# One product of 64 rows and 128 columns for two 64x64 products in a fused attention and MLP kernel

## The chip, the cores and the metric

The kernel runs on one core of a Trainium2 chip. The metric is the device time of one execution in microseconds. A core has a matrix engine (TensorE, PE in the profile), a vector engine (VectorE, DVE), a scalar engine (ScalarE, ACT), GpSimd (POOL) and a queue of transfers (SyncE, SP). A matrix product on TensorE is two instructions: a weight load, LDWEIGHTS, which puts the stationary operand into the 128x128 array (PEld in the profile), and MATMUL, which streams the columns of the moving operand through it (PE).

## What is computed

```python
q_n, k_n = rmsnorm(q, g_q), rmsnorm(k, g_k)            # (8, 12, 448, 64)
scores = matmul(q_n, k_n.T) / sqrt(64)
attn = exp(scores - max); attn = attn / sum(attn)
x = matmul(attn, v)                                    # -> (3584, 768)
h = x @ w_in                                           # first layer, 768 -> 2048
out = gelu_tanh(h) @ w_out                             # second layer, 2048 -> 768
```

There are 8 batches of 12 heads, 448 tokens and 64 values a head. Inputs and output are float32; the products are of bfloat16 operands with float32 sums.

## The kernel before

The kernel goes through the batches one after the other. For one batch it does an attention, which gives `xT` (768 by 448, transposed), and then the first layer with its gelu, which writes half of `g` (two batches of 448 tokens side by side). The second layer of tokens that are already in `g` is done in small pieces between the pieces of the next batch's attention, so that TensorE has work while ScalarE computes exponentials. Batch 0's attention is `first_attention`; batches 1 to 7 go through `attention(b, ...)`. What is left of the second layer after batch 7 is done in `final`.

Inside `attention` the order of TensorE's work is written out by hand in a string. A word `5r` takes five steps of the second layer; `u` is one unit of scores, `unit()` at L335; `s` is the sum of the exponentials by a product with ones, and `x` the product with `v`, both `products()` at L387. Batch 1 uses `SECOND`, batches 2 to 7 use `STEADY`:

```python
STEADY = (
    "5r u 11r uu 8r uu 8r 1r u 6r u 4r u 5r uu 6r su 5r u 3r u 2r 7r uxu 4r u 5r uu 1r s 7r u"
    " 3r uu 5r 16r x 11r s 5r x",
    ...
SECOND = (
    "u 8r uu 9r u 7r uu 10r u 3r u 5r u 2r u 4r us 6r u 3r u 1r u 6r xu 4r u 5r u 1r u"
    " 3r s 1r u 2r u 10r u 2r x 1r s 3r x",
```

Adjacent `r` words, such as `8r 1r`, make one run of steps. `STEADY` has 19 runs: it begins with one, right behind the first layer of the batch before, and each is followed by a `u`, an `s` or an `x`. `SECOND` has 22 runs, begins with a `u`, and each run is followed by a `u`, an `s` or an `x` too.

A unit makes the scores of 64 keys with 448 queries for two heads and two row halves: four products of 64 rows (the contraction) and 64 columns of stationary operand, each in its own quarter of the array. `products()` is cut in the same way. One step of the second layer (`quartered`, L495) is cut so too: the index `r` picks one half of the 128 contracted rows of block `f`, with its own output bank; the index `a` picks one half of the 128 tokens, with its own half of the output's partitions. The two products of one `r` have the same moving operand `wout[rs, f, lo:hi]`, of 384 or 192 columns. After all `f` the halves are swapped over the banks (`turn`), so each bank gets both halves of the contraction.

The first layer of batch 1 (`mm1_turn`, L537) is cut in the same way, with `xT` of 448 columns as the moving operand. The first layers of the other batches (L556 for batch 0, L625 and L652 for batches 2 to 7) and `final` (L914) use stationary operands of 128 rows and 128 columns. The profile writes these forms as 64\*64 and 128\*128. The transposes of batch 0 (L296) and the filler products (L269) are 128\*128 as well, and two small products for the gains (L1073) are 32\*128.

Of the kernel before, what the change touches and what calls it, by code (L numbers as in the profile page):

```python
# [17 lines left out]
def kernel(  # L18
# [11 lines left out]
    nc = tc.nc  # L30
    B, H, S, D = q.shape
# [7 lines left out]
    R = 64  # L39
# [23 lines left out]
    start = ctx.enter_context(ExitStack())  # L63
# [6 lines left out]
    def pair(name):  # L70
        rounds.append(rounds.pop(0))
        return rounds[-1]
# [34 lines left out]
    win = wts.tile([128, HP, d_ff], BF16)  # L107
    wout = wts.tile([128, nf, d_model], BF16)
# [5 lines left out]
    qT, xT = {}, {}  # L114
    g = gp.tile([128, nf, 2 * S], BF16, tag="g", name="g")
# [352 lines left out]
    def follows(mm):  # L468

        tc.add_manual_dep(  # L470
            nc.tensor.nop().ins, mm.ins.name,
            mybir.DependencyInfo(mybir.DependencyClass.Sync, mybir.DependencyReason.DATA),
        )

    def quartered(parts, finished, late=False):

        o = rounds.pop(0)
        half = nf // 2
        order = [(0, 0, nf), (1, 0, nf)]
        if late:
            order = [(0, 0, half), (1, 0, half), (1, half, nf), (0, half, nf)]
        steps = [(turn, f) for turn, lo, hi in order for f in range(lo, hi)]
        for n, (turn, f) in enumerate(steps):
            if n and turn != steps[n - 1][0]:
                follows(mm)
            for r in range(2):  # L490
                bank = (r + turn) % 2
                (i, lo, hi), rs = parts[bank], slice(r * D, (r + 1) * D)
                for a in range(2):
                    at = i * 128 + a * R
                    mm = nc.tensor.matmul(  # L495
                        o[a * R:(a + 1) * R, bank, :hi - lo], g[rs, f, at:at + R],
                        wout[rs, f, lo:hi],
                        start=(n == 0), stop=(n == len(steps) - 1),
                    )
            if n == len(steps) - 1:  # L500
                rounds.append(o)
                finished(o)
            yield
# [19 lines left out]
    def mm1_turn(b, i, turn, cs, begin=False, end=False):  # L523

        if begin:
            hs1[i] = [pair("hh"), None]
        elif hs1[i][1][0] != turn:
            follows(hs1[i][1][1])  # L530
        h = hs1[i][0]
        for c in cs:
            for r in range(2):
                j, rs = (r + turn) % 2, slice(r * D, (r + 1) * D)
                for a in range(2):
                    at = (2 * i + j) * 128 + a * R
                    mm = nc.tensor.matmul(  # L537
                        h[a * R:(a + 1) * R, j, :S], win[rs, c, at:at + R], xT[b][rs, c],
                        start=begin and c == cs[0], stop=end and c == cs[-1],
                    )  # L540
        hs1[i][1] = turn, mm
        if end:
            nc.scalar.activation(
                g[:, 2 * i:2 * i + 2, (b % 2) * S:(b % 2 + 1) * S], h[:, :, :S],
                AF.Gelu_apprx_tanh,
            )
# [182 lines left out]
    def attention(b, side, extra, ends):  # L729
# [12 lines left out]
        def second_layer():  # L742
            for k, parts in enumerate(tiles):
                def finished(o, k=k):
                    full[k] = o
                    made.add(("full", k))
                yield from quartered(parts, finished, late=b == 1 and k == 0)
# [76 lines left out]
        if b > 1:  # L824
            sevens[b] = Seven(b)
            sevens[b].early()
        else:
            mm1_turn(b, 0, 0, early, begin=True)
            mm1_turn(b, 1, 0, early, begin=True)
            mm1_turn(b, 0, 1, early)  # L830
            mm1_turn(b, 2, 0, early, begin=True)
            mm1_turn(b, 1, 1, early)
            mm1_turn(b, 2, 1, early)
# [237 lines left out]
    for j in range(2):  # L1071
        rs = slice(j * 32, (j + 1) * 32)
# [95 lines left out]
    for b in range(B):  # L1168
# [80 lines left out]
        for f in range((nf // 2, nf)[b] if b < 2 else 0):  # L1249
            i, part = f // 4 * 2, f % 4  # L1250
# [71 lines left out]
```

## Time and profile before

| | |
|---|---|
| median of 3 runs | 385.32 us (384.76 to 386.1) |
| the profiled execution's own time | 384.59 us |
| its span in the trace | 382.8 us |
| granted TensorE clock | 0.999 |
| busy share of the span: PE, PEld, DVE, ACT, POOL | 98%, 71%, 78%, 76%, 35% |
| TensorE instructions | 6508 MATMUL, 6508 LDWEIGHTS |
| of these L495, the second layer in the attentions | 3456 of each |
| of these L537, the first layer of batch 1 | 384 of each |

A busy matrix engine means that some product is in it; a product's record runs from its start until its last result is out, so records of products that follow each other overlap. How long a piece of work holds TensorE is therefore read from start to start, not from a record's duration.

### The profile page before, as it was taken

The page shows a single profiled execution, that of the slowest core. Times are in us where ns is not written, and L with a number is a line of the kernel's source. Part 1 is how long each engine was busy: PE and PEld are TensorE (multiplying, and loading weights), DVE is VectorE, ACT ScalarE, POOL GpSimd, SP SyncE. Part 2 cuts the span into 40 slices and gives each one's busy share as a digit, 9 for nine tenths or more (in the row PEclk, how much of TensorE's full clock was granted, in tenths as well). Part 3 has the DMA queues.
Part 4 walks back from the last instruction along what each step waited for, and adds up shares of the span by engine and source line. Part 5 has one row for each costly group of instructions (what it writes and reads, how often), then busy time and mean ns, then how long its engine had stood idle before and what let it go on. Part 6 is the DMA issues. An engine that isn't in the chain of part 4 may idle for free.

```text
span 382.8 us, 14538 instructions
## 1 busy us (share of the span) xinstructions
PE 374.9 (98%) x6508; PEld 273.6 (71%) x6508; DVE 299.4 (78%) x441; ACT 289.6 (76%) x358; POOL 134.1 (35%) x118
## 2 busy tenths in 40 slices
PE   8899999999999999999999999999999999999995
PEld 5565577677878858886678867788678866778563
DVE  4999969995999758895789956996588833899853
ACT  6995589777997689877897789966897659965500
POOL 5997504349203850057401861038400640000000
PEclk9999999999999999999999999999999999999999
DMA  8999999978913996259832897139553340220023
GB/s 255 324 236 210 210 238 235 275 152 190 245 48 77 223 203 112 59 109 260 184 90 53 193 252 117 45 89 222 112 98 84 74 96 15 74 63 3 2 61 105
DMA packets 64594, 54.48 MB, mean 142 GB/s; under 512 B 37652, under 2 KB 60436, under 8 KB 64532
## 3 DMA queue, kind: packets, MB, share of 16 engines
q1 hardware_dynamic: 54016, 41.04, 42.8%
q0 software_dynamic: 10128, 11.80, 18.5%
q8 instruction: 51, 0.84, 0.9%
q10 hardware_dynamic: 388, 0.72, 0.5%
q14 instruction: 11, 0.09, 0.1%
HBM read 45.61 MB, written 11.01 MB: 148 GB/s over the span
## 4 chain that ended last, share of the span: by engine, by line
PE 92%; ACT 5%; DMA 1%; DVE 0%; issue 0%; POOL 0%
PE t L495 33%; PE t L652 14%; PE t L625 13%; PE t L387 9%; PE t L335 8%; PE t L537 5%; PE t L914 5%; ACT ex L343 4%; PE t L556 4%; DMA rawq<-in_q_dram 1%; PE h L436 1%; PE tp L296 1%; PE o L387 0%; DVE ss L173 0%; POOL nrmq L278 0%
## 5 line engine op out<-in xcount | busy, mean ns | idle before, releaser
L343 ACT ACTIVATE ex<-t,shift 128x896 bf16<-128x896 f32 x168 | 156.7, 1013 | 2.9 <-PE t L335 2.2
L495 PE MATMUL t<-wout,g 64*64 64x384 bf16 (+1 forms) x3456 | 150.6, 305 | 0.0
L495 PEld LDWEIGHTS <-g 64*64 64x64 bf16 x3456 | 104.4, 107 | 29.2 <-issue 2.2
L335 PE MATMUL t<-qT,kT 64*64 64x448 bf16 x672 | 57.5, 351 | 1.4 <-ACT ex L343 0.6
L652 PE MATMUL t<-xT,win 128*128 128x448 bf16 x288 | 58.5, 353 | 0.0
L173 DVE TENSOR_REDUCE ss<-sq 128x14 f32<-128x896 f32 (+3 forms) x45 | 43.5, 995 | 18.5 <-ACT sq L162 16.1
L1035 POOL COPY mark<-es 1x1 bf16<-1x1 bf16 x7 | 1.2, 177 | 128.2 <-DVE es L362 119.8
L652 PEld LDWEIGHTS <-win 128*128 128x128 bf16 x288 | 27.7, 98 | 24.1 <-issue 2.1
L278 POOL TENSOR_TENSOR nrmq<-rawq,rinv 128x896 bf16<-128x896 f32 (+1 forms) x21 | 35.4, 1688 | 19.2 <-ACT rinv L205 10.6
L355 DVE TENSOR_TENSOR es<-ex 128x1792 bf16<-128x1792 bf16 x21 | 22.3, 1061 | 16.3 <-ACT ex L343 16.3
L278 POOL TENSOR_TENSOR nrmk<-rawk,rinv 128x896 bf16<-128x896 f32 (+1 forms) x21 | 34.6, 1647 | 0.0
L397 DVE STREAM_TRANSPOSE st<-t 128x448 f32<-128x448 f32 x42 | 24.8, 629 | 10.5 <-PE t L387 9.7
L387 PE MATMUL t<-ex,vb 64*64 64x448 bf16 x588 | 32.3, 350 | 0.0
L335 PEld LDWEIGHTS <-kT 64*64 64x64 bf16 x672 | 23.7, 106 | 9.4 <-issue 1.4
L625 PEld LDWEIGHTS <-win 128*128 128x128 bf16 x288 | 27.6, 98 | 2.7 <-issue 1.0
L658 ACT ACTIVATE g<-t 128x896 bf16<-128x896 f32 x24 | 22.0, 916 | 9.3 <-PE t L652 9.3
L387 PEld LDWEIGHTS <-vb 64*64 64x64 bf16 x672 | 23.3, 107 | 7.9 <-issue 1.2
L409 DVE STREAM_TRANSPOSE rb<-rc 128x896 f32<-128x896 f32 (+1 forms) x25 | 26.7, 1067 | 0.3
L636 ACT COPY xs<-t 128x896 f32<-128x896 f32 x18 | 16.3, 906 | 13.0 <-PE t L625 10.5
L422 DVE TENSOR_TENSOR xT<-t,rb 128x896 bf16<-128x896 f32 x21 | 22.8, 1086 | 0.9
L513 ACT COPY osb<-t 128x768 f32<-128x768 f32 (+1 forms) x18 | 12.6, 703 | 14.0 <-PE t L495 14.0
L164 POOL TENSOR_TENSOR sq<-rawk 128x896 f32<-128x896 f32 (+1 forms) x14 | 22.6, 1614 | 0.7 <-DMA rawk<-in_k_dram 0.7
(147 smaller groups left out, 529.3 us busy)
## 6 DMA issues: line engine op xcount, KB each, us to landing
rawq<-in_q_dram SPq DMA_DIRECT2D x22, 448.0 KB, 4.3
rawk<-in_k_dram SPq DMA_DIRECT2D x22, 448.0 KB, 5.7
out_dram<-osb SPq DMA_DIRECT2D x38, 192.0 KB, 2.9
vb<-in_v_dram POOLq DMA_DIRECT2D x6, 672.0 KB, 7.6
win<-in_moe_w_in_dram POOLq DMA_DIRECT2D x8, 384.0 KB, 11.6
out_dram<-osb SPq DMA_DIRECT2D x31, 96.0 KB, 2.5
wout<-in_moe_w_out_dram POOLq DMA_DIRECT2D x3, 768.0 KB, 18.0
vb<-in_v_dram POOLq DMA_DIRECT2D x2, 448.0 KB, 16.4
```

The source lines that it names most:

```text
L164: eng.tensor_mul(sq, raw, raw)
L173: nc.vector.reduce_sum(sss[b][:, seat(b, c), "qk".index(n), hs, ts], squares(b, c, n, hs, ts), axis=AX.X)
L278: eng.tensor_mul(nrms[n, b, c][:, ts].rearrange("p t a d -> p a t d"), raws[n, b, c][:, :, ts], root[:, :, ts].to_broadcast([P, 2, m, D]),)
L335: nc.tensor.matmul(sc[r * R:(r + 1) * R, a, :S], kT[rs, c, t, r], qT[b][rs, c, :, r], start=True, stop=True,)
L343: nc.scalar.activation(exs[b, c][:, t], scs.pop((b, c, t))[:, :, :S], AF.Exp, scale=scale, bias=shift)
L387: nc.tensor.matmul(o[r][a * D:(a + 1) * D], vb[b % 2][rs, 2 * c + a, i] if what else ones[rs], es[i][rs, a], start=(i == 0), stop=(i == n ...
L397: nc.vector.transpose(st[:, r].rearrange("p a b -> p (a b)"), o[r])
L409: nc.vector.transpose(oas["rb"][:, rs].rearrange("p r s -> p (r s)"), rc.to_broadcast([128, (rs.stop - rs.start) * m, 32]),)
L422: nc.vector.tensor_mul(xT[b][:, 2 * c:2 * c + 2], oas["o", c, 1][:, :, :S], oas["rb"])
L495: mm = nc.tensor.matmul(o[a * R:(a + 1) * R, bank, :hi - lo], g[rs, f, at:at + R], wout[rs, f, lo:hi], start=(n == 0), stop=(n == len(step ...
L625: nc.tensor.matmul(t[:, bank, n * QS:(n + 1) * QS], self.lhs[i][:, m, at:at + 128], self.rhs[i][:, m], start=i == owner and n == m == 0, s ...
L652: nc.tensor.matmul(h[:, j, :S], win[:, c, at:at + 128], xT[self.b][:, c], start=(c == 0), stop=(c == HP - 1),)
```

## The change

At two places the loop over `a` goes away. Where two products of 64 rows and 64 columns used the same moving operand, there is one product of 64 rows and 128 columns, which writes all 128 partitions of its bank. The loop over `r` stays, so a step is two products in place of four. The order of the steps among the units, sums and products, and all else, stays.

```diff
             for r in range(2):
                 bank = (r + turn) % 2
                 (i, lo, hi), rs = parts[bank], slice(r * D, (r + 1) * D)
-                for a in range(2):
-                    at = i * 128 + a * R
-                    mm = nc.tensor.matmul(
-                        o[a * R:(a + 1) * R, bank, :hi - lo], g[rs, f, at:at + R],
-                        wout[rs, f, lo:hi],
-                        start=(n == 0), stop=(n == len(steps) - 1),
-                    )
+                mm = nc.tensor.matmul(
+                    o[:, bank, :hi - lo], g[rs, f, i * 128:(i + 1) * 128], wout[rs, f, lo:hi],
+                    start=(n == 0), stop=(n == len(steps) - 1),
+                )
...
             for r in range(2):
                 j, rs = (r + turn) % 2, slice(r * D, (r + 1) * D)
-                for a in range(2):
-                    at = (2 * i + j) * 128 + a * R
-                    mm = nc.tensor.matmul(
-                        h[a * R:(a + 1) * R, j, :S], win[rs, c, at:at + R], xT[b][rs, c],
-                        start=begin and c == cs[0], stop=end and c == cs[-1],
-                    )
+                at = (2 * i + j) * 128
+                mm = nc.tensor.matmul(
+                    h[:, j, :S], win[rs, c, at:at + 128], xT[b][rs, c],
+                    start=begin and c == cs[0], stop=end and c == cs[-1],
+                )
```

The lines behind the edit move up: L495 becomes L493, L537 becomes L533, L556 becomes L552, L625 becomes L621, L652 becomes L648 and L914 becomes L910; L335 and L387 stay.

On TensorE, in batch 1's attention, a run of a single step (the word `1r` between two `u`) stands between two units. Before, with `t1` the output of the second layer, and `t3` and `t0` the scores of the unit ahead and the unit behind (the last part of a MATMUL row is the output's partitions by its columns):

```order
L335 MATMUL t3_894<-qT_845,kT_124 64x448
L495 LDWEIGHTS g_125
L495 MATMUL t1_101<-wout_120,g_125 64x384
L495 LDWEIGHTS g_125
L495 MATMUL t1_101<-wout_120,g_125 64x384
L495 LDWEIGHTS g_125
L495 MATMUL t1_101<-wout_120,g_125 64x384
L495 LDWEIGHTS g_125
L495 MATMUL t1_101<-wout_120,g_125 64x384
L335 LDWEIGHTS kT_124
L335 MATMUL t0_100<-qT_845,kT_124 64x448
```

The same place on TensorE after the change:

```order
L335 MATMUL t3_894<-qT_845,kT_124 64x448
L493 LDWEIGHTS g_125
L493 MATMUL t1_101<-wout_120,g_125 128x384
L493 LDWEIGHTS g_125
L493 MATMUL t1_101<-wout_120,g_125 128x384
L335 LDWEIGHTS kT_124
L335 MATMUL t0_100<-qT_845,kT_124 64x448
```

Four loads and four products of 64 columns became two loads and two products of 128 columns, at the same place between the same units; the units stay 64\*64.

Also on TensorE, batch 1's first layer begins right behind the last product with `v`. Before, with `t2` the layer's output:

```order
L387 LDWEIGHTS vb1_122
L387 MATMUL t1_101<-ex_1335,vb1_122 64x448
L537 LDWEIGHTS win_119
L537 MATMUL t2_893<-xT_1321,win_119 64x448
L537 LDWEIGHTS win_119
L537 MATMUL t2_893<-xT_1321,win_119 64x448
```

And after:

```order
L387 LDWEIGHTS vb1_122
L387 MATMUL t1_101<-ex_1207,vb1_122 64x448
L533 LDWEIGHTS win_119
L533 MATMUL t2_893<-xT_1193,win_119 128x448
L533 LDWEIGHTS win_119
L533 MATMUL t2_893<-xT_1193,win_119 128x448
```

The layer's four products of a step became two here too, and it now begins with a form that differs from the product ahead of it. At its other end a run of the second layer follows, whose form changed with it.

Counted over all of TensorE's program, two products that follow each other differ in form 36 times before: 17 times from 64\*64 to 128\*128, 17 times back, and once each way between 32\*128 and 128\*128. After, those stay (in 5 of them the 64\*64 is now 64 rows by 128 columns), and 267 changes between 64\*64 and 64 rows by 128 columns are new: 37 in each attention of batches 2 to 7 (19 at the ends of runs, 18 at the beginnings) and 44 in batch 1's, and 1 at the beginning of batch 1's first layer.

## The prediction

> **What bounds the kernel now.** The page's busy times come first, then its chain of waits.
>
> ```profile
> PE 374.9 (98%) x6508; PEld 273.6 (71%) x6508; DVE 299.4 (78%) x441; ACT 289.6 (76%) x358; POOL 134.1 (35%) x118
> PE 92%; ACT 5%; DMA 1%; DVE 0%; issue 0%; POOL 0%
> ```
>
> TensorE has a product in it for 98% of the span, and 92% of the chain that ended last lies on it. An average can hide a stage with another limit, so I read busy time by stretches: batch 4's attention, its first layer, batch 5's attention, then batch 1's attention and batch 1's first layer. The columns are the stretch, its length, and busy time with instruction counts for PE, PEld, DVE, ACT and POOL.
>
> ```profile
> 182.78:209.72 26.94, 26.94 (x694) 20.40 (x693) 22.58 (x31) 24.13 (x29) 3.90 (x5) 1.00 0.46 105
> 209.72:227.04 17.32, 17.32 (x136) 12.65 (x132) 12.58 (x15) 12.78 (x17) 12.38 (x9) 1.00 0.88 210
> 227.04:254.05 27.01, 27.01 (x694) 20.47 (x693) 22.65 (x31) 24.14 (x29) 3.97 (x5) 1.00 0.45 99
> 50.47:75.76 25.29, 25.29 (x581) 18.80 (x580) 22.51 (x40) 22.78 (x29) 6.67 (x8) 1.00 1.04 255
> 75.76:94.11 18.35, 18.35 (x391) 13.60 (x386) 15.46 (x27) 12.94 (x19) 12.66 (x9) 1.00 0.80 172
> ```
>
> TensorE is never empty in the stages that the change touches. ScalarE is next, with 24.13 us of 26.94. So time added on TensorE there has no cover and goes to the end of the kernel whole, and time removed there could bring at most 2.8 us an attention before ScalarE binds.
>
> Is TensorE also full, with columns streaming all the time? A busy record can't tell, so I take starts from the timeline (start, duration, line, form, count), first of a run in batch 4's attention, then of the final layer.
>
> ```profile
> 199.31 0.39 PE L335 MATMUL t<-qT,kT 64*64 64x448 bf16 x4
> 199.50 1.01 PE L495 MATMUL t<-wout,g 64*64 64x384 bf16 x20
> ```
>
> ```profile
> 359.98 1.30 PE L914 MATMUL t<-wout,g 128*128 128x384 bf16 x7
> ```
>
> The 20 products of L495 are five steps of four. The groups of the profile by line and form give one record's duration:
>
> ```profile
> L495 PE MATMUL t<-wout,g 64*64 64x384 bf16 x2688 | 132.4, 323 | 0.0
> L495 PE MATMUL t<-wout,g 64*64 64x192 bf16 x768 | 19.3, 243 | 0.0
> L914 PE MATMUL t<-wout,g 128*128 128x384 bf16 x48 | 8.3, 326 | 0.0
> L914 PE MATMUL t<-wout,vb 128*128 128x192 bf16 x16 | 1.5, 246 | 0.0
> ```
>
> Five steps lie within 1.01 us, of which the last four-product step takes about 0.36 (0.323 and a few hundredths between its first and last start), so a step is (1.01 - 0.36)/4 = 0.163 us. The full-array products of 384 columns come every (1.30 - 0.326)/6 = 0.162 us. A step of four quarter products thus already costs what one full-array product of that width costs: the quarters run beside each other, and the columns stream without a gap. The unit shows the same: 199.50 - 199.31 = 0.19 us for four products of 448 columns.
>
> **What the change removes.** It halves L495's 3456 and L537's 384 loads and products. Worth in time: next to nothing, since a step still streams 384 (or 192, or 448) columns. 864 steps of L495 could fall from 0.163 to the 0.162 of the full array, 0.9 us. TensorE's idle time ahead of L335, in all 1.4 us by the next row, is the only other slack. So the gain is between 0 and 2.3 us, and I take 0.
>
> ```profile
> L335 PE MATMUL t<-qT,kT 64*64 64x448 bf16 x672 | 57.5, 351 | 1.4 <-ACT ex L343 0.6 <-DVE kT L305 0.5 <-DVE shift L1083 0.3
> ```
>
> No trace shows a 64-row, 128-column product, so its step is bounded from both sides. If the two row halves run beside each other it is 0.162; one behind the other, 0.324. The nearest rows are the two 32\*128 products of L1073, in different row groups, in the timeline and then in the groups by form:
>
> ```profile
> 7.49 0.19 PE L1073 MATMUL t<-gbf,rows 32*128 32x32 bf16 x2 [0.66 <-DVE nrmq L278]
> 7.61 0.28 PE L296 MATMUL tp<-ident,nrmq 128*128 128x128 bf16 x2
> ```
>
> ```profile
> L1073 PE MATMUL t<-gbf,rows 32*128 32x32 bf16 x2 | 0.2, 184 | 0.7 <-DVE nrmq L278 0.7
> ```
>
> Both lie within 0.19 us although one takes 0.184, so they started together. I take 0.162.
>
> A load of 128 columns must also fit under a step. The narrow steps of 192 columns are the test, 192 of them (768 products by four). In the final layer a full-array product of 192 columns, each with its own 128-column load, comes every (1.5 - 0.246)/15 = 0.084 us, so the load keeps up. I take 0. The Trainium skill, "TensorE: Matmul & The Clock Gate", section "LDWEIGHTS (loading the stationary operand)", speaks against the change here: it prices a load by its columns at 1.2 a nanosecond, so 128 columns are 107 ns where 64 are 53. By that page alone, narrow steps paced by their load would cost 192 x (107 - 84) ns, an estimate of 4.4 us more; the row above, with loads of the same width at 84 ns, is against it.
>
> **What the change adds.** It puts 267 new changes of form on TensorE: 6 x 37 in the attentions of batches 2 to 7, 44 in batch 1's, and 1 into batch 1's first layer. What a change of form costs is seen where the trace has them. In batch 0's attention one unit (64\*64) and seven filler products (128\*128) alternate, and nothing waits for another engine between them:
>
> ```profile
> 10.89 0.38 PE L335 MATMUL t<-qT,kT 64*64 64x448 bf16 x4
> 11.21 0.58 PE L269 MATMUL o<-const-bfloat16-1.0 128*128 128x128 bf16 x7
> 11.72 0.38 PE L335 MATMUL t<-qT,kT 64*64 64x448 bf16 x4
> 12.04 0.58 PE L269 MATMUL o<-const-bfloat16-1.0 128*128 128x128 bf16 x7
> 12.55 0.38 PE L335 MATMUL t<-qT,kT 64*64 64x448 bf16 x4
> ```
>
> One round is 11.72 - 10.89 = 0.83 us. Its work, without changes, is 0.19 for the unit and 7 x 0.06 = 0.42 for the fillers (seven lie within 0.58, of which the last is 0.222 by the next row: 0.36/6 = 0.06). That leaves 0.83 - 0.61 = 0.22 us for two changes, 0.11 each.
>
> ```profile
> L269 PE MATMUL o<-const-bfloat16-1.0 128*128 128x128 bf16 x35 | 2.9, 222 | 0.0
> ```
>
> The unit alone tells it too: from its start to what comes behind is 11.21 - 10.89 = 0.32 us, against 0.19 in the run at 199.31, 0.13 more. At the beginning of batch 5's attention, where the full-array first layer gives way to the second layer, the timeline has
>
> ```profile
> 225.81 1.30 PE L652 MATMUL t<-xT,win 128*128 128x448 bf16 x6
> 227.04 1.01 PE L495 MATMUL t<-wout,g 64*64 64x384 bf16 x20
> 227.88 0.36 PE L335 MATMUL t<-qT,kT 64*64 64x448 bf16 x4
> ```
>
> Six products at the 0.19 that 448 columns take hold TensorE for 1.14 us; the run starts after 1.23, 0.09 more. The five steps behind take 0.84, where 5 x 0.163 is 0.82: the first step pays 0.02 to 0.03 on top, its weights not having been loaded beforehand. Together 0.115 us. The loads say why:
>
> ```profile
> 209.71 0.11 PEld L652 LDWEIGHTS <-win 128*128 128x128 bf16 x2 [0.36 <-issue]
> ```
>
> No load was issued for 0.36 us at the change, and the load starts only as the product does: TensorE empties first, and then nothing is ready.
>
> All these rows change the row count as well (64 to 128), and L1073 to L296 changes rows alone, from 32 to 128: 7.61 - 7.49 = 0.12 us for products of 32 columns, which is about 0.10 of emptying. None changes columns alone. So the price for 64\*64 against 64\*128 lies between 0 (if only rows matter) and 0.13. I take 0.115, between the round's 0.11 and the unit's 0.13, because the emptying is the same 0.09 to 0.11 whichever row counts change and in both directions. The Trainium skill, "TensorEngine Tiling (Array Packing)", section "Key Properties", says that a change of tiling mode drains TensorE while a change of tile doesn't, and lists 64x64 and 64x128 as different configurations; it gives no price, and the rows give one for other pairs only.
>
> The sum: 267 x 0.115 = 30.7 us, with no cover: 37 x 0.115 = 4.3 us in an attention of 26.94, which makes TensorE's lead over ScalarE wider. The other engines and the queue get later work, never earlier, and no wait is added. The profiled execution, 384.59 us, becomes 415.3. It lies 0.73 under the median of the runs, 385.32, so I forecast 416.0 us.
>
> **The rivals.** First, a change of columns alone is free. For it: no row shows such a change, and quarters that share rows are filled beside each other today. Against it: the steadiness of the price. It would give 385.3 less the 0 to 2.3 us above, 383.0 to 385.3: not slower. The price per change decides: below 1.2/267 = 0.004 us nothing is measured (0.3% of the time, 1.2 us, is about what a measurement can tell). 9%, of which 3% faster by over 0.3% and 6% within.
>
> Second, a partial price: TensorE needn't empty, but loads can't go ahead of a change, so each pays only the 0.02 to 0.03 of an unprepared first step: 267 x 0.025 = 6.7, 392.0 us. Against it is the 0.36 us without loads, which shows both at once. 8%.
>
> Third, the row halves don't run beside each other: 672 wide steps of 0.162, 192 of 0.084 and 96 of L537 at 0.19 are added, 109 + 16 + 18 = 143 us, and with the changes 559 us. The L1073 row is against it. 3%.
>
> **How the numbers follow.** The forecast has 80%. Its range: the price at its lowest reading, 0.09 x 267 = 24.0, less the gain of 2.3, is 384.6 + 21.7 = 406.3; at its highest, the whole 0.12 from L1073 to L296 and 0.025 for an unprepared step, 0.145 x 267 = 38.7, it is 423.3. With the median's offset, 407.0 to 424.0. The other cases lie outside it and hold the 20% that may be left out. Faster 0.03, same 0.06, slower 0.91.
>
> **What would show it.** In the changed profile, the run and the units around it should start 0.32 us behind a unit's start where it is 0.19 now; steps within a run should still be 0.163 apart; batch 4's attention should be about 31.2 us, batch 1's about 30.4, batch 1's first layer 18.4 to 18.5, and the full-array first layers unchanged at 17.3. Loads should pause at every change of form, and ScalarE should wait for L335. If attentions keep 27 us, the price is wrong; if steps are 0.32 apart, the overlap is.

## The result, and the profile after

The changed kernel takes 413.84 us (median of 4 runs, 413.7 to 414.0) where the kernel before takes 385.71 us in the same comparison: 1.073 times as long, 95% interval 1.071 to 1.076. Its profiled span is 412.0 us, 29.2 us over the span before.

The page's busy times and shares of the chain, after:

```profile
PE 403.3 (98%) x4588; PEld 227.7 (55%) x4588; DVE 301.9 (73%) x441; ACT 296.5 (72%) x358; POOL 134.2 (33%) x118
PE 92%; ACT 5%; DMA 1%; issue 1%; DVE 0%; POOL 0%; ACTq 0%
```

TensorE is as busy as before by share, with 1920 products fewer: busy time doesn't show that it now pauses 267 times more. The stretches do. These are batch 4's attention, its first layer, batch 1's attention and batch 1's first layer, with the columns as before.

```profile
195.04:226.17 31.13, 31.13 (x438) 15.03 (x437) 23.41 (x32) 25.30 (x29) 4.10 (x5) 1.00 0.38 87
226.17:243.50 17.33, 17.33 (x137) 12.66 (x134) 12.50 (x14) 12.66 (x17) 12.27 (x9) 1.00 0.87 219
50.07:79.95 29.88, 29.88 (x386) 12.72 (x385) 23.67 (x42) 23.58 (x29) 7.53 (x9) 1.00 0.92 219
79.95:98.12 18.17, 18.17 (x196) 9.35 (x194) 13.88 (x25) 12.88 (x18) 12.42 (x9) 1.00 0.74 176
```

An attention of batches 2 to 7 grew from the 27.01 us of the row before to 31.13, by 4.12; six of them make 24.7 us. For batch 1 the same ends, from first product to first product, give these rows before:

```profile
50.33:75.41 25.08, 25.08 (x578) 18.71 (x579) 22.30 (x40) 22.60 (x28) 6.32 (x8) 1.00 1.04 256
75.41:93.91 18.50, 18.50 (x391) 13.65 (x387) 15.81 (x27) 13.23 (x20) 12.81 (x9) 1.00 0.79 175
```

So batch 1's attention grew from 25.08 to 29.88, by 4.80. That is 4.12/37 = 0.111 us a change in the one and 4.80/44 = 0.109 in the other. The full-array first layer kept its 17.3 us, and batch 1's own first layer went from 18.50 to 18.17: before, one of its 96 steps took 0.53 us in place of 0.19, a pause that the changed kernel does not have. 24.7 + 4.8 - 0.3 is the whole 29.2 us; other stages differ by up to 0.3 us either way and cancel. The timeline shows where in an attention it lies; this is batch 4's, some 18 us in:

```profile
213.46 0.82 PE L493 MATMUL t<-wout,g 64*128 64x384 bf16 x8
214.21 0.38 PE L335 MATMUL t<-qT,kT 64*64 64x448 bf16 x4
214.53 0.99 PE L493 MATMUL t<-wout,g 64*128 64x384 bf16 x10
215.44 0.57 PE L335 MATMUL t<-qT,kT 64*64 64x448 bf16 x8
```

From the unit to the run behind it is 214.53 - 214.21 = 0.32 us, where it was 0.19. The run has five steps (10 products), and the next unit starts 0.91 us later, where five steps took 5 x 0.163 = 0.82. Within the run nothing changed: (0.99 - 0.33)/4 = 0.165 a step. The loads of the same place:

```profile
213.46 0.44 PEld L493 LDWEIGHTS <-g 64*128 64x128 bf16 x8 [0.36 <-issue]
214.21 0.11 PEld L335 LDWEIGHTS <-kT 64*64 64x64 bf16 x4 [0.32 <-issue]
214.53 0.60 PEld L493 LDWEIGHTS <-g 64*128 64x128 bf16 x10 [0.20 <-issue]
215.44 0.14 PEld L335 LDWEIGHTS <-kT 64*64 64x64 bf16 x8 [0.32 <-issue]
```

Each group of loads starts at the very time of its products and not ahead of them, with 0.20 to 0.36 us of no load in front, put down to no engine ("issue"). The groups by form show it as a sum, the first two rows before, the next two after:

```profile
L495 PEld LDWEIGHTS <-g 64*64 64x64 bf16 x3456 | 104.4, 107 | 29.2 <-issue 2.2
L335 PEld LDWEIGHTS <-kT 64*64 64x64 bf16 x672 | 23.7, 106 | 9.4 <-issue 1.4 <-DVE kT L305 1.2 <-DVE qT L309 0.2
L493 PEld LDWEIGHTS <-g 64*128 64x128 bf16 x1728 | 71.7, 94 | 65.8 <-issue 28.9 <-PE t L335 7.5 <-PE t L493 0.2
L335 PEld LDWEIGHTS <-kT 64*64 64x64 bf16 x672 | 17.4, 104 | 36.1 <-issue 32.7 <-DVE kT L305 1.2 <-DVE qT L309 0.2
```

The pauses of "issue" ahead of these loads went from 2.2 to 28.9 us and from 1.4 to 32.7. ScalarE now waits for the units too (first row before, then after), and the wide products' own records are as long as those of the quarters were:

```profile
L343 ACT ACTIVATE ex<-t,shift 128x896 bf16<-128x896 f32 x168 | 156.7, 1013 | 2.9 <-PE t L335 2.2
L343 ACT ACTIVATE ex<-t,shift 128x896 bf16<-128x896 f32 x168 | 161.8, 1007 | 20.0 <-PE t L335 19.2
L533 PE MATMUL t<-xT,win 64*128 64x448 bf16 x192 | 18.3, 349 | 0.0
L493 PE MATMUL t<-wout,g 64*128 64x192 bf16 x384 | 18.9, 243 | 0.0
```

### The profile page after: what moved, and what is told of

The parts are those of the page before. It is cut to its first block, busy times and chain, and to the rows that moved or that the text cites. A ratio compares the mean times of both kernels' runs of the same rounds, so it can differ in the third digit from the quotient of the medians.

```text
span 412.0 us, 10697 instructions
## 1 busy us (share of the span) xinstructions
PE 403.3 (98%) x4588; PEld 227.7 (55%) x4588; DVE 301.9 (73%) x441; ACT 296.5 (72%) x358; POOL 134.2 (33%) x118
## 3 DMA queue, kind: packets, MB, share of 16 engines
q0 software_dynamic: 10128, 11.80, 17.3%
## 4 chain that ended last, share of the span: by engine, by line
PE 92%; ACT 5%; DMA 1%; issue 1%; DVE 0%; POOL 0%; ACTq 0%
PE t L493 34%; PE t L648 13%; PE t L621 12%; PE t L335 10%; PE t L387 9%; PE t L910 4%; PE t L533 4%; ACT ex L343 4%; PE t L552 4%; DMA rawq<-in_q_dram 1%; PE h L436 1%; PE tp L296 0%; PE o L387 0%; POOL nrmq L278 0%; DVE ss L173 0%
## 5 line engine op out<-in xcount | busy, mean ns | idle before, releaser
L343 ACT ACTIVATE ex<-t,shift 128x896 bf16<-128x896 f32 x168 | 161.8, 1007 | 20.0 <-PE t L335 19.2
L493 PE MATMUL t<-wout,g 64*128 64x384 bf16 (+1 forms) x1728 | 148.7, 306 | 0.0
L493 PEld LDWEIGHTS <-g 64*128 64x128 bf16 x1728 | 71.7, 94 | 65.8 <-issue 28.9
L335 PE MATMUL t<-qT,kT 64*64 64x448 bf16 x672 | 58.0, 365 | 1.4 <-ACT ex L343 0.6
L648 PE MATMUL t<-xT,win 128*128 128x448 bf16 x288 | 58.5, 353 | 0.0
L278 POOL TENSOR_TENSOR nrmq<-rawq,rinv 128x896 bf16<-128x896 f32 (+1 forms) x21 | 35.5, 1689 | 24.7 <-ACT rinv L205 15.4
L648 PEld LDWEIGHTS <-win 128*128 128x128 bf16 x288 | 27.7, 98 | 24.1 <-issue 2.1
L335 PEld LDWEIGHTS <-kT 64*64 64x64 bf16 x672 | 17.4, 104 | 36.1 <-issue 32.7
L387 PE MATMUL t<-ex,vb 64*64 64x448 bf16 x588 | 31.7, 351 | 0.0
L621 PEld LDWEIGHTS <-win 128*128 128x128 bf16 x288 | 27.6, 98 | 2.9 <-issue 1.3
L387 PEld LDWEIGHTS <-vb 64*64 64x64 bf16 x672 | 19.2, 106 | 12.5 <-issue 3.8
L358 DVE TENSOR_TENSOR es<-es,ex 128x1792 bf16<-128x1792 bf16 x21 | 22.7, 1080 | 0.7
```

The lines of the kernel that those rows point to most:

```text
L278: eng.tensor_mul(nrms[n, b, c][:, ts].rearrange("p t a d -> p a t d"), raws[n, b, c][:, :, ts], root[:, :, ts].to_broadcast([P, 2, m, D]),)
L335: nc.tensor.matmul(sc[r * R:(r + 1) * R, a, :S], kT[rs, c, t, r], qT[b][rs, c, :, r], start=True, stop=True,)
L343: nc.scalar.activation(exs[b, c][:, t], scs.pop((b, c, t))[:, :, :S], AF.Exp, scale=scale, bias=shift)
L358: nc.vector.tensor_add(es, es, ex[:, 4:6])
L387: nc.tensor.matmul(o[r][a * D:(a + 1) * D], vb[b % 2][rs, 2 * c + a, i] if what else ones[rs], es[i][rs, a], start=(i == 0), stop=(i == n ...
L493: mm = nc.tensor.matmul(o[:, bank, :hi - lo], g[rs, f, i * 128:(i + 1) * 128], wout[rs, f, lo:hi], start=(n == 0), stop=(n == len(steps) - 1),
```

## The experiments

The theory to test: each change of form costs about 0.11 us, the wide products nothing, and it is the whole array that empties. The rivals: a wide product costs something itself (its load, or halves that don't overlap); a change waits only for the cells that the other form still uses.

**The first layer of batch 1 alone.** From the kernel before, only `mm1_turn` is changed.

```diff
-                for a in range(2):
-                    at = (2 * i + j) * 128 + a * R
-                    mm = nc.tensor.matmul(
-                        h[a * R:(a + 1) * R, j, :S], win[rs, c, at:at + R], xT[b][rs, c],
+                at = (2 * i + j) * 128
+                mm = nc.tensor.matmul(
+                    h[:, j, :S], win[rs, c, at:at + 128], xT[b][rs, c],
...
```

> Only batch 1's first layer has the wide products; the second layer stays in four quarters. It has 2 new changes of form (into the layer and out of it). If the whole cost is the changes of form, at 0.11 us each: 385.7 + 0.2 = 385.9 us, no measurable difference, with the 96 wide steps still 0.189 us apart. If a wide product costs something by itself (its load, its halves not overlapped), the layer's 18.5 us grow by more than 0.3 us.

Measured: 386.06 us against 385.39, ratio 1.0019 (1.0004 to 1.0034). The stretch of the layer in this kernel, from its first product to the first one behind it:

```profile
77.60:95.86 18.26, 18.26 (x195) 9.25 (x192) 14.34 (x26) 13.01 (x19) 11.75 (x7) 1.00 0.80 173
```

It is 18.26 us, against 18.22 for the same layer in quarters in the next experiment. 96 wide steps cost nothing by themselves. The interval holds the 0.2 us of two changes and a little more. The waits of TensorE in this profile name a pause of 1.8 us near the end of batch 1's attention, at products that the edit doesn't touch. The next experiment and the last one (one form through the first layers) have such a pause at the same place. The rows are of this experiment, the next and the last:

```profile
PE t L387 <- issue: 1.8, 1, 1.8
PE t L387 <- issue: 0.9, 1, 0.9
PE t L387 <- issue: 1.5, 1, 1.5
```

The last one leaves batch 1's attention as it was, and the kernels before and after have no such pause there. So I don't count it to the edit; what causes it stays open.

**Only the narrow steps wide.** From the kernel before, with `m` the columns of a product in `quartered`:

```diff
-                for a in range(2):
-                    at = i * 128 + a * R
+                m = 128 if hi - lo < HD else R
+                for at in range(0, 128, m):
                     mm = nc.tensor.matmul(
-                        o[a * R:(a + 1) * R, bank, :hi - lo], g[rs, f, at:at + R],
+                        o[at:at + m, bank, :hi - lo], g[rs, f, i * 128 + at:i * 128 + at + m],
```

> Only the second layer's steps of 192 columns (192 of the 864 steps, in batches 2 to 7) have the wide products: 36 new changes of form, 6 an attention. By changes of form at 0.11 us: 385.7 + 4.0 = 389.7 us, each of these attentions 0.66 us longer (27.0 to 27.7). By a load of 128 columns that paces narrow steps (107 against 81 ns), 192 x 0.026 = 5.0 us more, 394.7 us, and narrow steps 0.107 apart.

Measured: 389.22 us against 385.39, ratio 1.0102 (1.0066 to 1.0138), 3.8 us for 36 changes, 0.106 each. Batch 4's attention, then batch 1's first layer, which this edit leaves in quarters:

```profile
184.67:212.37 27.70, 27.70 (x630) 19.72 (x629) 23.18 (x32) 24.27 (x29) 4.10 (x5) 1.00 0.45 103
76.36:94.58 18.22, 18.22 (x392) 15.06 (x387) 14.74 (x26) 13.14 (x20) 12.07 (x8) 1.00 0.80 170
```

The attention is 27.70, 0.69 more for 6 changes, 0.115 each. The timeline of its end has a run of eleven narrow wide steps:

```profile
209.07 1.08 PE L495 MATMUL t<-wout,g 64*128 64x192 bf16 x22
210.08 0.38 PE L387 MATMUL t<-es,ones 64*64 64x448 bf16 x4
```

Eleven steps lie within 1.08 us, of which the last is 0.243: (1.08 - 0.243)/10 = 0.084 apart, not 0.107. The 128-column load does not pace them.

**Every second step wide.** The same edit with another condition:

```diff
+                m = 128 if n % 2 else R
```

> Every second step of the second layer has the wide products, the others the four quarters: half as many wide products as in the changed kernel, but 864 new changes of form in place of 267. If the cost goes with the number of changes: 864 x 0.11 = 95 us, 481 us. If it goes with the number of wide products or of wide steps, it is half the 28 us or less, 399 us.

Measured: 482.37 us in one run, 97.0 us over the kernel before in that comparison, for 864 changes: 0.112 each. With half the wide products the cost is more than three times that of the changed kernel. It goes with the changes; over 36, 267 and 864 of them the price is 0.106, 0.105 and 0.112 us.

**Mixed halves.** The same edit again:

```diff
+                m = 128 if r == 0 else R
```

> Within each step of the second layer the upper row half is one wide product and the lower row half two products of 64 columns; the forms differ, but no cell of the array is shared between them. If a change of form empties the whole array, whatever rows it is in, each step has two changes and its halves can't overlap: a wide-column step is about 0.16 + 0.093 + 0.16 + 0.095 (+ 0.024) = 0.51 to 0.535 us in place of 0.163, a narrow one 0.35 to 0.375 in place of 0.081, and the kernel 687 to 708 us. If only the cells that are in use by the other form have to be waited for, the halves overlap as before, changes cost only where a run meets a unit, and it is 386 to 415 us.

Measured: 968.0 us in one run. Neither number, but the side is plain: the halves don't overlap. The timeline's first run, and a later one:

```profile
50.51 4.43 PE L495 MATMUL t<-wout,g 64*128 64x384 bf16 x24
54.60 0.72 PE L335 MATMUL t<-qT,kT 64*64 64x448 bf16 x8
55.25 7.87 PE L495 MATMUL t<-wout,g 64*128 64x384 bf16 x27
62.60 0.90 PE L335 MATMUL t<-qT,kT 64*64 64x448 bf16 x4
```

Rows of one line stand merged here under their first form. In the first run eight steps take 54.60 - 50.51 = 4.09 us, 0.51 each, as the emptying of the whole array says, and not 0.163. So a form change in the upper half holds up the lower half, though they share no cell. The second run's nine steps take 7.35 us, 0.82 each. What changed between the two runs is in the page's row of the granted clock, and in the stretches (the third number from the end of each):

```profile
PEclk9965559555567557695555865557755559555589
```

```profile
50.51:52.69 2.18, 2.18 (x16) 0.80 (x13) 2.15 (x6) 2.17 (x2) 0.00 (x0) 1.00 1.21 200
55.50:66.00 10.50, 10.50 (x40) 2.69 (x39) 1.15 (x5) 2.64 (x3) 0.00 (x0) 0.50 0.15 55
```

After the first few microseconds of such steps the clock was granted at one half, and over the kernel at 0.647. A step grew by 0.82 - 0.51 = 0.31 us, about what its two streams of 0.16 us gain when the clock halves, so by this estimate the emptying itself hardly grew. The 687 to 708 us had been worked out for a full clock.

**The upper half only.** To narrow down what took the clock, the kernel before with the lower row half of the second layer's steps left out:

```diff
-            for r in range(2):
+            ends = [m for m, (t, _) in enumerate(steps) if t == turn]
+            for r in range(1):
...
-                        start=(n == 0), stop=(n == len(steps) - 1),
+                        start=(n == ends[0]), stop=(n == ends[-1]),
```

> The kernel before, with the lower row half of the second layer's steps in the attentions left out: two 64*64 products a step in place of four, no new changes of form. It is to tell what halved the granted clock where the mixed halves ran (0.647 in all). If half-empty steps alone do it, the clock falls below 0.9 here and steps of 384 columns are 0.32 us apart, 440 us or more. If it takes the pauses at the changes as well, the clock stays at 1.0, steps at 0.163 and the kernel at 385 us.

Measured: 384.24 us in one run, clock 0.998. The groups by form, and the timeline of a run of eight steps:

```profile
L496 PE MATMUL t<-wout,g 64*64 64x384 bf16 x1344 | 131.2, 323 | 0.0
```

```profile
227.73 1.46 PE L496 MATMUL t<-wout,g 64*64 64x384 bf16 x16
```

(1.46 - 0.323)/7 = 0.162 us a step. Half-empty steps without pauses keep the clock, and so do 864 pauses between steps that use the full array (every second step wide: clock 1.000). Mixed halves have half-empty products and pauses together, but also two pauses a step, twice as many. Whether it takes both, or only so many pauses, is not shown.

**One form through the first layers.** If changes cost 0.11 us, the kernel before still pays for those between attentions and full-array first layers. Here the first layers of batches 2 to 7 are cut into quarters with swapped banks too:

```diff
-            for bank in range(2):
-                for n in range(2):
-                    at = (bank * 2 + n) * 128
-                    for m in ms:
-                        nc.tensor.matmul(
-                            t[:, bank, n * QS:(n + 1) * QS],
-                            self.lhs[i][:, m, at:at + 128], self.rhs[i][:, m],
+            for k, (n, turn) in enumerate(((0, 0), (0, 1), (1, 1), (1, 0))):
+                if k:
+                    follows(mm)
+                for m in ms:
+                    for r in range(2):
+                        bank, rs = (r + turn) % 2, slice(r * D, (r + 1) * D)
+                        for a in range(2):
+                            at = (bank * 2 + n) * 128 + a * R
+                            mm = nc.tensor.matmul(
+                                t[a * R:(a + 1) * R, bank, n * QS:(n + 1) * QS],
+                                self.lhs[i][rs, m, at:at + R], self.rhs[i][rs, m],
...
```

> The kernel before, with the first layers of batches 2 to 7 cut into quarters too, so that no form changes between an attention and its first layer: 10 changes between 128*128 and 64*64 fewer (12 and 12 in place of 17 and 17), the same columns streamed. By 0.11 us a change: 1.1 us faster, 384.3 us, ratio 0.997, with first layers still 17.2 to 17.3 us and attentions 0.1 to 0.2 us shorter. If the quarters cost something that the full array doesn't (four loads under 0.096 us of 224 columns), the first layers grow and the gain is gone or more: 1% slower for each 0.65 us of a layer.

Measured: 436.44 us, ratio 1.132 (1.129 to 1.135), a clear miss. Batch 4's attention and its first layer:

```profile
201.22:228.07 26.85, 26.85 (x696) 20.64 (x692) 21.84 (x29) 23.95 (x29) 3.21 (x4) 1.00 0.36 73
228.07:254.05 25.98, 23.60 (x535) 12.24 (x528) 14.22 (x16) 13.14 (x17) 13.14 (x9) 1.00 0.80 170
```

The attention is 0.15 us shorter, as expected, but the layer takes 25.98 us in place of 17.32. The waits at the layer's two lines, of the load queue for products of the same line:

```profile
  PE t L629: 49.3, 162
```

```profile
  PE t L661: 18.0, 36
```

The code does not let the two row halves write one bank at the same time: at each swap of the banks (`follows`) the next loads wait until the last product is out. There are 198 swaps, and 50.8 us more, about 0.26 us each. The chain that ended last shows single swaps in batch 4's first layer:

```profile
238.03 0.80 PE t L629 x24
238.83 0.04 issue
238.88 0.51 PE t L629 x12
239.39 0.04 issue
239.43 0.51 PE t L629 x12
```

Three steps (12 products) more take 0.80 - 0.51 = 0.29 us, 0.097 a step of 224 columns, and in the kernel before the chain has 2.30 us for 24 full-array products of that width, 0.096 each. So the quarters cost nothing themselves. But from swap to swap three steps take 239.43 - 238.88 = 0.55 us, 0.26 more than 0.29. In batch 1's first layer the code puts another tile's products between the two turns, and its steps stay 0.19 us apart; I did not do so here. Whether a version with hidden swaps would win the 1.1 us was not tried.

## Why the prediction was right

The forecast was 416.0 us with a range of 407 to 424, and 413.84 came out.

- That TensorE is the bound with no cover: right. All the time added in the attentions came out at the end, and ScalarE's wait ahead of L343 rose from 2.9 to 20.0 us.
- That the change saves nothing: right. Steps stay at 0.163 to 0.165 us, narrow ones at 0.084, and batch 1's first layer alone, with half its loads and products gone, brought no time (18.26 us, against 18.22 in quarters).
- That the row halves run beside each other: right; the third rival's 0.32 us steps did not come.
- That a change of columns alone costs as much as the other changes, the step without a row of its own: right. The unit's 0.32 us and the run's 0.09 us are the numbers read from 64\*64 against 128\*128. The first rival, a free change, and the second, only an unprepared load, are out. Mixed halves, with 0.51 us a step in place of 0.163, showed that it is the whole array that empties. The Trainium skill, "TensorEngine Tiling (Array Packing)", section "Key Properties", has the rule that a change of tiling mode drains TensorE, and under "Available Configurations" 64x64 and 64x128 are two modes. The trace agrees: 0.32 us from a unit to a run where it was 0.19.
- The price of 0.115 us was a little high: 29.2/267 = 0.109 by the spans, and 28.1/267 = 0.105 by the medians. In medians the forecast was 385.32 + 30.7, and what came is 385.71 + 28.1. So the price made it 2.6 us too high, the reference 0.4 us too low, and 2.2 us of difference are left.
- Batch 1's attention was to be about 30.4 us and took 29.88. Its row before, 25.29 us, ran to 75.76, but the layer's first product starts at 75.41: from first product to first product it was 25.08, and 44 changes at 0.109 give 29.88.
- Batch 1's first layer was to be 18.4 to 18.5 us and took 18.17. The layer before held a pause that is not the change's: with the layer left in quarters, the second experiment has 18.22.
- The 4.4 us by the Trainium skill's price of a load, in "TensorE: Matmul & The Clock Gate", section "LDWEIGHTS (loading the stationary operand)", did not come: a 128-column load's record is 94 ns in the changed kernel, and narrow steps stand 0.084 us apart.

## What to carry to other kernels

Count how often two neighbouring products differ in the rows and columns that they use of the array, and price each such change at about 0.11 us of TensorE before merging or splitting products; interleaved work should keep one form even if that doubles the number of instructions. Four quarter products that stream beside each other already cost what one full-array product does (0.163 against 0.162 us at 384 columns), so fewer instructions are no gain as long as the columns set the pace. Where row halves share an output bank by turns, put another tile's work between the turns.

## What had not been expected of the hardware

The granted clock can fall while TensorE's record is full: with mixed halves PE was busy for 99% of the span, and the clock was 0.647 in the mean and 0.50 for long stretches. Half-empty steps without pauses (0.998), and half as many pauses with a full array (1.000), did not lower it. And a load queue that must wait at each swap of banks cost 0.26 us a swap, more than twice a change of form.
